# Mirrored matrix rows by way of DRAM, values by head in DRAM, and the order of the attention loads

## The chip, the cores and the metric

The kernel runs on one core of a Trainium2 chip. The metric is the device time of one execution in microseconds; the time before is the median of three runs. A profile of one further execution shows what each engine did: TensorE (PE, with its weight loads PEld), VectorE (DVE), ScalarE (ACT), GpSimd (POOL) and SyncE (SP), which here does nothing but issue DMAs. Line numbers (L941) are those of the kernel before.

## The reference

Two independent halves of 2048 tokens by 448 features each, whose results stand side by side in the output. Half A is a Fourier mixing layer, half B is attention with 16 heads of 28 features:

```python
# A: y = Re(DFT_seq(DFT_hidden(x))), with the four DFT matrices as inputs
a = einsum("bsd,ed->bse", x, dft_hid_re);  b = einsum("bsd,ed->bse", x, dft_hid_im)
y = einsum("ts,bse->bte", dft_seq_re, a) - einsum("ts,bse->bte", dft_seq_im, b)
# B: qkv = x @ wqkv, heads of 28
scores = einsum("bhqd,bhkd->bhqk", q, k) * 28 ** -0.5
o = einsum("bhqk,bhkd->bhqd", softmax(scores), v);  out = o (heads joined) @ wo
# result: concatenate([A, B], axis=-1), 2048 x 896, float32
```

The sequence matrices `dft_seq_re` and `dft_seq_im` (2048 x 2048 each, 16 MB) are inputs and not constants.

## The kernel before, in words

**The halves.** For B, queries, keys and values are computed first from `xb` and `wqkv`, each as a high and a low part, so that float32 precision is kept. Queries and keys go to a DRAM tensor `qk_d`, values to `v_d` (line 373), and each head reads back what it needs: keys in four pieces of 512 tokens (`head_loads`, L1183), queries in four pieces (`load_q`, L1197), values in one load. For every head the sixteen rows of score tiles (`kt` 0 to 15) are made 128 keys by 512 queries at a time (L1284), ACT exponentiates them (L1292), and PE multiplies them with the values (`quad`, L1261, matmuls at L1267). The row `kt` 0 of a head comes early (`first_tiles`, L1213): its maxima over the keys, made on DVE and POOL (L1230 to L1256), are subtracted inside all later rows of the head, so L1284 of a head cannot start before them. Buffers: five for key pieces, eight for query pieces (two heads), two for values.

**The sequence matrices.** A uses the symmetry of the DFT matrices to do a quarter of the work. Since the matrices are inputs, the kernel also checks on the chip that they do have that symmetry; if not, a slow general path runs at the end (it does not run with these inputs). The check reads both matrices whole, while attention runs, into six buffers `raw` of 128 x 1024: `rows_check` compares rows of one half with the other, `tokens_check` compares rows with the rows in descending order, `column_check` compares the first columns. The work is subtractions on DVE or POOL (`against`, L953) and a maximum on DVE (`largest`, L899).

**The descending rows.** `tokens_check` needs, for each of four blocks b and each matrix, rows in descending order. `Turned` (L935) reads them straight from the matrix with a negative row step, in four DMAs of 128 x 256 elements that POOL issues (L941). For block 0 the first row of each of the four groups is another one; it is read by two small DMAs over the same buffer, which wait for the four large ones (L946).

**The order of the work.** The whole program is written out by a planner (`Schedule`): each task has an engine, a key, a duration and what it depends on, and for each engine in turn the ready task with the lowest key is taken as soon as its buffers are free in the plan. Every engine then runs its list in that order on the chip. `soon` lowers the key by which a task is picked, but not the key by which buffers are handed out in turn. A task on SP is a DMA; the plan lets eight be in flight, and models their landing. `begun(key)` ties a load of the check to the head that the plan expects at that time: it may not be issued before that head reaches its fifth row of scores (`opened`, L1291).

**Values.** `values` (L775) makes them for eight heads at a time, 128 tokens after 128 tokens. Each result is copied with a one and three zeros behind each head's 28 columns (32 in all) into its own `kept` buffer, and stored by one DMA of 128 KB (L795). `head_loads` reads a head's 32 columns of all tokens (L1191).

Of the kernel before, what the change touches and what calls it, by code (L numbers as in the profile page):

```python
# [11 lines left out]
F32 = mybir.dt.float32  # L12
# [10 lines left out]
H = 16  # L23
# [12 lines left out]
SLACK_K, EARLY = 2.5, 8.0  # L36
# [3 lines left out]
T_FAR = 13.0  # L40
# [313 lines left out]
def tile_kernel(ctx, tc, xa, wre, wim, wd, xb, wqkv, wo, out):  # L354
# [18 lines left out]
    v_d = dram.tile([P, NT, H * VW], F32, name="vd")  # L373
# [401 lines left out]
    def values(ready, half):  # L775
        v_done[half] = []
        cols = slice(half * HV * DH, (half + 1) * HV * DH)
        for c in range(NC):
            for t in range(4):
                tok = slice(c * CH + t * P, c * CH + (t + 1) * P)  # L780
                o, pair = early_bank(), kept_s.slot()
                vs = lambda pair=pair: pair.t[:, 0, :HV * VW]
# [6 lines left out]
                def put(o=o, vs=vs):  # L789
                    v3 = vs().rearrange("p (h d) -> p h d", h=HV)  # L790
# [143 lines left out]

    class Turned(Stack):  # L935


        def __init__(self, part, b, key):
            self.raw = raw = raw_s.slot()
            src = (wre, wim)[part]  # L940
            at = lambda rows, cols, off, ap: far_dma(key, lambda: nc.gpsimd.dma_start(self.t[rows, cols], bass.AP(  # L941
                tensor=src.tensor, offset=src.offset + off, ap=[[tile_n, 4], *ap, [1, cols.stop - cols.start]])), T_FAR, d=0.7, deps=begun(key), use=[raw])
            q = H1 // 4
            self.ld = [at(slice(0, P), slice(i * q, (i + 1) * q), H1 + i * q + (P - 32 * b) * row_n, [[-row_n, 32]]) for i in range(4)]
            if not b:
                at = lambda cols, off: far_dma(key, lambda: nc.gpsimd.dma_start(self.t[0:P:32, cols], bass.AP(  # L946
                    tensor=src.tensor, offset=src.offset + off, ap=[[tile_n, 4], [1, cols.stop - cols.start]])), 3.0 + SLACK, d=0.6, deps=self.ld[:4], use=[raw])
                self.ld += [at(slice(0, H1 - P), H1 + P), at(slice(H1 - P, H1), 0)]
# [234 lines left out]
    def head_loads(h):  # L1183
        KT[h] = [kt_s.slot() for c in range(NC)]
        for c in range(NC):
            k = KT[h][c]
            got_k[h, c] = [dma(begins[h] - 34 - EARLY + (20 + c * P_H / NC if c else 0), lambda k=k, c=c: rows_of(
                k.t, 1, h * 2 * DH + DH, c * CH, (c + 1) * CH),
                size=84, extra=X_ROWS, n=2, slack=SLACK_K, deps=[*rows_ready(h, c, DH), *clears], use=[k])]
# [7 lines left out]
    def load_q(h, c, q):  # L1197
        return [dma(begins[h] - 33 - EARLY + c, lambda: rows_of(q.t, 0, h * 2 * DH, c * CH, (c + 1) * CH),
                    size=84, extra=X_ROWS, n=2, slack=SLACK_K, deps=[*rows_ready(h, c, 0), *clears], use=[q])]
# [290 lines left out]
def any_scores(tc, qk_d, v_d, on_d, wo, out, ks, qs, vs, kept, banks, new):  # L1490
# [20 lines left out]
    with tc.For_i(0, H, 1) as h:  # L1511
        with tc.For_i(0, S, CH) as c0:
# [16 lines left out]
            with tc.For_i(0, S, CH) as k0:  # L1529
                rows(k, h * 2 * DH + DH, (0, 0, 1), k0)  # L1530
                nc.gpsimd.dma_start(v, v_d[:, bass.ds(k0 // P, 4), bass.ds(h * VW, VW)])
# [85 lines left out]
```

## Time and profile before

| | |
|---|---|
| median of three runs | 743.26 us (742.86 to 743.95) |
| the profiled execution | 745.1 us, of which its span 743.5 us |
| granted TensorE clock over the span | 0.978 |
| busy | PE 710.5, ACT 610.9, DVE 507.3, POOL 375.8 us |
| DMA packets | 116160, of which 54470 under 512 bytes; 127.80 MB |
| DMA queue of SP | 109300 packets, 120.75 MB |
| DMA queue of POOL | 6784 packets, 6.14 MB |
| HBM | 96.64 MB read, 32.69 MB written |

The span is the time from the first to the last instruction in the trace. Busy time of PE is pipelined matmul time whose ends are modelled. A row of the stage tables names a stretch of the span and the busy time in it; a row of the chain of waits names when, for how long and on what the work that ended last was held up, followed back from the end.

### The profile page before, as it was taken

Reading aid. Unit: us, or ns where it says so; the run is one execution under the profiler, and the core shown is the slowest. Engines: PE = TensorE matmul, PEld = TensorE weight load, DVE = VectorE, ACT = ScalarE, POOL = GpSimd, SP = SyncE. Lnnn points to the kernel's source line nnn. Section 1 sums busy time; section 2 is a strip of 40 time slices with the busy share of each in tenths; the row PEclk is TensorE's granted clock in tenths of the full one; section 3 lists DMA queues with packets and bytes.
Section 4 is the critical chain, followed back from the end, with each engine's and each line's share of the span. In section 5 each row is a group of like instructions: output and inputs, shape, how many; then the busy total and the mean of one; then the engine's idle time right before and its main releaser. Section 6 shows DMA issues by size and latency. Waiting matters only on the chain.

```text
span 743.5 us, 12892 instructions
## 1 busy us (share of the span) xinstructions
PE 710.5 (96%) x4147; PEld 399.0 (54%) x4147; DVE 507.3 (68%) x864; ACT 610.9 (82%) x1232; POOL 375.8 (51%) x367
## 2 busy tenths in 40 slices
PE   9899999989999998899999999989989999999886
PEld 7697544444555544355545554535445554545765
DVE  6558637658868578687799776839888927423741
ACT  6315999968899989699999999979988999999141
POOL 7303314556464175553665356554898525547800
PEclk9999999998999999899999999989999999999989
DMA  8758539975779996888778599666352414232464
GB/s 289 251 196 221 147 80 224 193 162 151 169 200 242 257 192 177 200 216 217 203 195 228 151 243 220 161 194 200 103 141 78 101 50 124 62 107 51 109 190 181
DMA packets 116160, 127.80 MB, mean 172 GB/s; under 512 B 54470, under 2 KB 80728, under 8 KB 116084
## 3 DMA queue, kind: packets, MB, share of 16 engines
q1 hardware_dynamic: 109300, 120.75, 61.3%
q0 software_dynamic: 6784, 6.14, 3.7%
q8 instruction: 35, 0.57, 0.3%
q14 instruction: 41, 0.34, 0.2%
HBM read 96.64 MB, written 32.69 MB: 174 GB/s over the span
## 4 chain that ended last, share of the span: by engine, by line
PE 68%; ACT 9%; DMA 7%; POOL 6%; DVE 5%; issue 2%; SPq 1%; POOLq 0%; DVEq 0%; ACTq 0%
PE bank L1284 25%; PE bank L1267 25%; PE bank L687 10%; ACT kept L1292 7%; PE bank L867 3%; PE bank L1451 2%; PE bank L729 2%; DMA raw<-wre 2%; PE bank L1225 2%; DMA q<-qkd 1%; DMA kept<-kept 1%; POOL raw L953 1%; POOL kept L1256 1%; DMA kept<-ond 1%; DMA raw<-wim 1%
## 5 line engine op out<-in xcount | busy, mean ns | idle before, releaser
L1292 ACT ACTIVATE kept<-bank 128x512 f32<-128x512 f32 x960 | 499.7, 682 | 29.8 <-PE bank L1284 27.6
L1284 PE MATMUL bank<-q,k 98*128 98x512 f32 x960 | 304.5, 419 | 14.1 <-ACT kept L1292 8.0
L1284 PEld LDWEIGHTS bank<-q,k 98*128 98x128 f32 x960 | 174.1, 191 | 149.7 <-ACT kept L1292 106.3
L1267 PE MATMUL bank<-kept,v 128*32 128x512 f32 x2048 | 252.3, 611 | 0.0
L953 POOL TENSOR_TENSOR raw<-raw,raw 128x1024 f32<-128x1024 f32 (+3 forms) x54 | 112.1, 2081 | 53.8 <-DMA raw<-wre 29.6
L1267 PEld LDWEIGHTS bank<-kept,v 128*32 128x32 f32 x2048 | 54.4, 110 | 120.0 <-issue 114.3
L899 DVE TENSOR_REDUCE far<-raw 128x1 f32<-128x1024 f32 (+2 forms) x78 | 86.0, 1112 | 23.3 <-POOL raw L953 20.6
L1254 POOL CAST q<-mb 1x512 fp32r<-1x512 f32 x38 | 31.2, 830 | 109.4 <-DVE mb L1251 76.9
L1230 DVE STREAM_TRANSPOSE mb<-bank 128x512 f32<-128x512 f32 x64 | 43.9, 702 | 39.3 <-PE bank L1225 24.7
L1229 ACT ACTIVATE kept<-bank 128x512 f32<-128x512 f32 x64 | 39.5, 657 | 26.2 <-PE bank L1225 22.9
L1330 POOL TENSOR_TENSOR kept<-kept 128x512 f32<-128x512 f32 x16 | 20.8, 1301 | 77.6 <-DVE kept L1325 58.5
L1258 ACT ACTIVATE kept<-kept 128x512 f32<-128x512 f32 x64 | 46.0, 755 | 10.1 <-POOL kept L1256 5.0
L687 PE MATMUL bank<-big,whi 128*128 128x512 f32 x132 | 47.7, 402 | 1.7 <-DVE big L457 1.7
L1256 POOL TENSOR_TENSOR kept<-kept,mb 128x512 f32<-128x512 f32 x33 | 46.2, 1408 | 4.6 <-DVE mb L1251 1.6
L1251 DVE STREAM_TRANSPOSE mb<-am 128x512 f32<-128x512 f32 x64 | 42.9, 695 | 1.5 <-POOL q L1254 0.5
L1231 DVE TENSOR_REDUCE qm<-mb 128x16 f32<-128x512 f32 x64 | 41.7, 668 | 0.5
L687 PE MATMUL bank<-wd,big 128*128 128x224 f32 x288 | 41.8, 274 | 0.0
L687 PEld LDWEIGHTS bank<-wd,big 128*128 128x128 f32 x288 | 39.2, 191 | 3.4 <-issue 0.8
L953 DVE TENSOR_TENSOR raw<-raw,raw 128x1024 f32<-128x1024 f32 (+2 forms) x30 | 35.2, 1178 | 0.7 <-DMA raw<-wim 0.6
L1256 DVE TENSOR_TENSOR kept<-kept,mb 128x512 f32<-128x512 f32 x31 | 34.8, 1131 | 0.2
L687 PEld LDWEIGHTS bank<-big,whi 128*128 128x128 f32 x132 | 24.6, 189 | 12.5 <-issue 4.2
L1225 PE MATMUL bank<-q,k 84*128 84x512 f32 x64 | 27.6, 433 | 3.2 <-ACT kept L1292 2.3
(173 smaller groups left out, 788.3 us busy)
## 6 DMA issues: line engine op xcount, KB each, us to landing
raw<-wre SPq DMA_DIRECT2D x64, 256.0 KB
raw<-wim SPq DMA_DIRECT2D x64, 256.0 KB
qkd<-kept SPq DMA_DIRECT2D x40, 256.0 KB
k<-qkd SPq DMA_DIRECT2D x64, 112.0 KB
q<-qkd SPq DMA_DIRECT2D x64, 112.0 KB
kept<-xb SPq DMA_DIRECT2D x16, 256.0 KB
vd<-kept SPq DMA_DIRECT2D x32, 128.0 KB
v<-vd SPq DMA_DIRECT2D x16, 256.0 KB
```

The costliest lines, as they stand in the source:

```text
L687: nc.tensor.matmul(o.t[:, :cols], w(), x(), start=(i == 0), stop=(i == n - 1))
L899: far_done.append(dve(key, lambda: nc.vector.tensor_reduce(far[rows, part, n:n + 1], t(), axis=AX.X if len(t().shape) == 2 else AX.XY, op= ...
L953: return sch.add(d, at, lambda g: eng[g].tensor_tensor(xv(), xv(), yv(), op=op), deps=[*x.ld, *y.ld, *deps], use=[x.raw, y.raw])
L1225: m = pe(key, lambda e, o=o, q=q: nc.tensor.matmul(o.t, KT[h][0].t[:KR, :P], q.t[:KR, :], start=True, stop=True), deps=[*lq, *got_k[h, 0], ...
L1230: t = dve(key, lambda o=o, tm=tm: nc.vector.transpose(tm.t, o.t), 0.73, deps=[m], acq=[tm], use=[o], lock=[o], own=RAW_S)
L1231: rs.append(dve(key, lambda tm=tm, c=c: nc.vector.tensor_reduce(qm.t[:, 0, c * NT:(c + 1) * NT], tm.t.rearrange("p (j r) -> p j r", r=32), ...
L1251: t = dve(key, lambda mb=mb, c=c: nc.vector.transpose(mb.t, f32(am.t)[:, c * NT:(c + 1) * NT].unsqueeze(2).to_broadcast([P, NT, 32])), 0.7 ...
L1256: sh = sch.add({"DVE": 1.15, "POOL": 1.4}, key, lambda e, s=s, mb=mb: eng[e].tensor_tensor(s.t, s.t, mb.t, op=ALU.add), deps=[t, made[c]], ...
L1258: shown.append(act(key, lambda s=s: nc.scalar.activation(s.t, s.t, AF.Exp, scale=SCALE), ACT_S, deps=[sh], use=[s.pair]))
L1267: nc.tensor.matmul(o.t[c * VW:(c + 1) * VW, :], VT[h].t[:, kt // 4, kt % 4, :], tiles[c].t, start=(kt == 0), stop=(kt == NT - 1))
L1284: m = pe(key, lambda e, o=o, q=q, kt=kt: nc.tensor.matmul(o.t, KT[h][kt // 4].t[:KM, kt % 4 * P:(kt % 4 + 1) * P], q.t[:KM, :], start=True ...
L1292: es[h, kt].append(act(key - 20, lambda o=o, p=p: nc.scalar.activation(p.t, o.t, AF.Exp, scale=SCALE), deps=[m], use=[o, p.pair]))
```

## The change

**Mirrors.** A new function `mirror` makes, for each of the two sequence matrices, a copy of 4 x 128 rows of 1024 elements in DRAM (`t_d`), in descending order. Four DMAs that SP issues do it, each with 16 x 127 runs of 64 elements (256 bytes), so that the runs of a row lie on different DMA engines; two small ones fill the first row of each group. Their keys are 60 and 110 us. `Turned` then reads its block as four plain loads of 32 rows each, issued by SP after the mirror has landed. POOL issues none of these loads any more.

**Values by head.** `v_d` is ordered by partition, head, tile and column. Four results share one `kept` buffer and are stored by one DMA of 512 KB in runs of 512 bytes; a head's load is 128 runs of 2 KB.

**Loads of attention.** Key, query and value loads get `soon=PRIOR` (40 us); `EARLY`, which took 8 us off the keys of the key and query loads, becomes 0. The lines left out adapt the slow path.

```diff
-SLACK_K, EARLY = 2.5, 8.0
+SLACK_K, EARLY, PRIOR = 2.5, 0.0, 40.0
-T_FAR = 13.0
+MIRROR_AT = 60.0, 110.0
-    v_d = dram.tile([P, NT, H * VW], F32, name="vd")
+    v_d = dram.tile([P, H, NT, VW], F32, name="vd")
...
+            pair, put_all = kept_s.slot(), []
+            v4 = lambda pair=pair: pair.t.rearrange("p a b -> p (a b)").rearrange("p (h t d) -> p h t d", h=HV, t=4)
             for t in range(4):
...
-                b = dve(key - 45, put, 0.55, deps=[end], use=[o, pair])
-                v_done[half].append(dma(key - 20, lambda vs=vs, c=c, t=t: nc.sync.dma_start(
-                    v_d[:, 4 * c + t, half * HV * VW:(half + 1) * HV * VW], vs()), 128, deps=[b], use=[pair]))
+                put_all.append(dve(key - 45, put, 0.55, deps=[end], use=[o, pair]))
+            v_done[half].append(dma(key - 20, lambda v4=v4, c=c: nc.sync.dma_start(
+                v_d[:, half * HV:(half + 1) * HV, 4 * c:4 * c + 4, :].rearrange("p h t d -> p h (t d)"),
+                v4().rearrange("p h t d -> p h (t d)")), 512, deps=put_all, use=[pair]))
...
+    t_d = [dram.tile([4, P, H1], F32, name=f"mirror{i}") for i in range(2)]
+    mirrored = [[], []]
+    def mirror(part, key):
+        src, dst, n = (wre, wim)[part], t_d[part], H1 // 16
+        for a in range(4):
+            mirrored[part].append(dma(key + 6 * a, lambda a=a: nc.sync.dma_start(
+                bass.AP(tensor=dst.tensor, offset=dst.offset + (a * P + 1) * H1, ap=[[n, 16], [H1, P - 1], [1, n]]),
+                bass.AP(tensor=src.tensor, offset=src.offset + a * tile_n + H1 + (P - 1) * row_n, ap=[[n, 16], [-row_n, P - 1], [1, n]])),
+                900, 1.0, deps=begun(key)))
+        for c0, c1, off in ((0, H1 - P, H1 + P), (H1 - P, H1, 0)):
+            mirrored[part].append(dma(key, lambda c0=c0, c1=c1, off=off: nc.sync.dma_start(
+                bass.AP(tensor=dst.tensor, offset=dst.offset + c0, ap=[[P * H1, 4], [1, c1 - c0]]),
+                bass.AP(tensor=src.tensor, offset=src.offset + off, ap=[[tile_n, 4], [1, c1 - c0]])), 16, 1.0, deps=begun(key)))
...
-            at = lambda rows, cols, off, ap: far_dma(key, lambda: nc.gpsimd.dma_start(self.t[rows, cols], bass.AP(
-                tensor=src.tensor, offset=src.offset + off, ap=[[tile_n, 4], *ap, [1, cols.stop - cols.start]])), T_FAR, d=0.7, deps=begun(key), use=[raw])
...
+            self.ld = [dma(key, lambda a=a: nc.sync.dma_start(self.t[32 * a:32 * a + 32], t_d[part][a, 32 * b:32 * b + 32]),
+                           128, slack=SLACK, deps=[*begun(key), *mirrored[part]], use=[raw]) for a in range(4)]
...
-            got_k[h, c] = [dma(begins[h] - 34 - EARLY + ..., size=84, extra=X_ROWS, n=2, slack=SLACK_K, deps=..., use=[k])]
+            got_k[h, c] = [dma(begins[h] - 34 - EARLY + ..., size=84, extra=X_ROWS, n=2, slack=SLACK_K, soon=PRIOR, deps=..., use=[k])]
...
-            v.t.rearrange("p c t d -> p (c t) d"), v_d[:, :, h * VW:(h + 1) * VW]), extra=1.0, deps=v_done[h // HV], use=[v])]
+            v.t.rearrange("p c t d -> p (c t) d"), v_d[:, h]), soon=PRIOR, deps=v_done[h // HV], use=[v])]
...
+        mirror(part, MIRROR_AT[part])
```

The query loads (`load_q`) change as the key loads do, and `mirror` is called in the loop over the two matrices, between `rows_check` and `tokens_check`.

More of the change, by code (lines that the diff above doesn't have):

```diff
@@ L778, in values @@
         for c in range(NC):
+            pair, put_all = kept_s.slot(), []
+            v4 = lambda pair=pair: pair.t.rearrange("p a b -> p (a b)").rearrange("p (h t d) -> p h t d", h=HV, t=4)
             for t in range(4):
                 tok = slice(c * CH + t * P, c * CH + (t + 1) * P)
-                o, pair = early_bank(), kept_s.slot()
-                vs = lambda pair=pair: pair.t[:, 0, :HV * VW]
+                o = early_bank()
                 seq = products(lambda k: lz(x_h, k, tok), lambda k: lz(x_l, k, tok), lambda: lz(x_3, tok),
@@ L787, in values, with put @@
                             {3 * k: [xb_ready[c, k], ready[k], *ready[4:][:k // 3]] for k in range(4)}, v_last)
-                def put(o=o, vs=vs):
-                    v3 = vs().rearrange("p (h d) -> p h d", h=HV)
+                def put(o=o, t=t, v4=v4):
+                    v3 = v4()[:, :, t]
                     nc.vector.tensor_copy(v3[:, :, :DH], o.t[:, :HV * DH].rearrange("p (h d) -> p h d", h=HV))
@@ L939, in __init__ @@
             self.raw = raw = raw_s.slot()
-            src = (wre, wim)[part]
-            at = lambda rows, cols, off, ap: far_dma(key, lambda: nc.gpsimd.dma_start(self.t[rows, cols], bass.AP(
-                tensor=src.tensor, offset=src.offset + off, ap=[[tile_n, 4], *ap, [1, cols.stop - cols.start]])), T_FAR, d=0.7, deps=begun(key), use=[raw])
[L943 to L948, printed above, removed]
+            self.ld = [dma(key, lambda a=a: nc.sync.dma_start(self.t[32 * a:32 * a + 32], t_d[part][a, 32 * b:32 * b + 32]),
+                           128, slack=SLACK, deps=[*begun(key), *mirrored[part]], use=[raw]) for a in range(4)]
     sub_if = lambda yes: ALU.subtract if yes else ALU.add
@@ L1188, in head_loads @@
                 k.t, 1, h * 2 * DH + DH, c * CH, (c + 1) * CH),
-                size=84, extra=X_ROWS, n=2, slack=SLACK_K, deps=[*rows_ready(h, c, DH), *clears], use=[k])]
+                size=84, extra=X_ROWS, n=2, slack=SLACK_K, soon=PRIOR, deps=[*rows_ready(h, c, DH), *clears], use=[k])]
         v = VT[h] = v_s.slot()
         got_v[h] = [dma(begins[h] - 4, lambda: nc.sync.dma_start(
-            v.t.rearrange("p c t d -> p (c t) d"), v_d[:, :, h * VW:(h + 1) * VW]), extra=1.0, deps=v_done[h // HV], use=[v])]
+            v.t.rearrange("p c t d -> p (c t) d"), v_d[:, h]), soon=PRIOR, deps=v_done[h // HV], use=[v])]
         flat = lambda: v.t.rearrange("p c t d -> p (c t d)")
@@ L1198, in load_q @@
         return [dma(begins[h] - 33 - EARLY + c, lambda: rows_of(q.t, 0, h * 2 * DH, c * CH, (c + 1) * CH),
-                    size=84, extra=X_ROWS, n=2, slack=SLACK_K, deps=[*rows_ready(h, c, 0), *clears], use=[q])]
+                    size=84, extra=X_ROWS, n=2, slack=SLACK_K, soon=PRIOR, deps=[*rows_ready(h, c, 0), *clears], use=[q])]
     before = {}
@@ L1530, in any_scores @@
                 rows(k, h * 2 * DH + DH, (0, 0, 1), k0)
-                nc.gpsimd.dma_start(v, v_d[:, bass.ds(k0 // P, 4), bass.ds(h * VW, VW)])
+                nc.gpsimd.dma_start(v, v_d[:, bass.ds(h, 1), bass.ds(k0 // P, 4), :].rearrange("p o t d -> p (o t) d"))
                 for kt in range(4):
```

## The prediction

> **What bounds the kernel now.** I read the page first, then the busy time of every engine head by head (a head runs from its first exponential of line 1292 to the next head's), then the chain of waits in the heads that stand out.
>
> ```profile
> span 743.5 us, 12892 instructions
> PE 710.5 (96%) x4147; PEld 399.0 (54%) x4147; DVE 507.3 (68%) x864; ACT 610.9 (82%) x1232; POOL 375.8 (51%) x367
> ```
>
> The share of PE says little, since its ends are modelled. The heads say more. Columns: stretch, its length, then busy time of PE, PEld, DVE, ACT and POOL, the granted clock, the DMA share and GB/s.
>
> ```profile
> 102.60:136.50 33.90, 33.87 (x194) 14.73 (x193) 24.21 (x35) 33.73 (x70) 13.10 (x11) 1.00 0.77 184
> 136.50:180.50 44.00, 40.07 (x224) 19.32 (x224) 30.49 (x48) 35.56 (x71) 27.88 (x23) 0.92 0.72 163
> 180.50:218.70 38.20, 38.17 (x241) 20.21 (x241) 29.47 (x52) 34.46 (x70) 18.20 (x10) 1.00 0.75 187
> 294.60:340.50 45.90, 40.89 (x216) 19.68 (x217) 35.50 (x51) 37.02 (x75) 24.70 (x18) 0.93 0.81 201
> 340.50:378.10 37.60, 36.69 (x215) 18.59 (x213) 28.32 (x41) 35.13 (x72) 20.89 (x21) 1.00 0.84 206
> 378.10:415.80 37.70, 37.70 (x216) 19.03 (x216) 34.87 (x44) 36.07 (x75) 20.31 (x14) 1.00 0.75 203
> 452.50:496.00 43.50, 40.68 (x213) 19.47 (x212) 31.57 (x48) 36.65 (x74) 28.55 (x28) 0.92 0.70 181
> 533.70:576.20 42.50, 39.91 (x243) 20.85 (x241) 34.89 (x59) 37.14 (x77) 39.05 (x39) 0.96 0.43 119
> sum 623.00, PE 605.72 PEld 309.49 DVE 442.60 ACT 573.35 POOL 334.41; mean PE 37.86 PEld 19.34 DVE 27.66 ACT 35.83 POOL 20.90
> ```
>
> The sixteen heads fill 623.0 of the 743.5 us. A quiet head takes 37.7 us with ACT busy for 36.1 of it, so there ACT sets the pace and nothing that this change touches can shorten it. Four heads are longer: head 2 (from 136.5) by 6.3 us, head 6 (294.6) by 8.2, head 10 (452.5) by 5.8, head 12 (533.7) by 4.8. In all four ACT was busy no longer than about 37 us and the granted clock is 0.92 to 0.96: PE and ACT both stood still. These 25.1 us are the room for any change outside ACT.
>
> Head 2, by the chain of waits (start, length, what):
>
> ```profile
> 151.69 8.23 DMA raw<-wre
> ...
> 161.64 2.40 POOL raw L953
> ...
> 165.28 2.05 DVE kept L1256
> ...
> 167.36 0.63 ACT kept L1258
> ...
> 168.53 1.77 PE bank L1284 x3
> ```
>
> ```profile
> POOL raw L941 <- DVE far L899: 10.0, 4, 3.9
> ...
> POOL raw L946 <- DMA raw<-wre: 8.2, 1, 8.2
> ...
> POOL raw L946 <- DMA raw<-wim: 6.8, 1, 6.8
> ```
>
> POOL issues the mirrored loads of the check (line 941), and for the first block of each matrix it must then wait for them before it issues the two small ones on top (line 946). While it stands, the check's subtraction (L953), and the maxima behind it (L1254, L1256) that let the next head's scores start, stand too. The same wait for the second matrix, 6.8 us, lies in the head from 340.5, which shows no excess: it costs nothing.
>
> Head 6 has another chain:
>
> ```profile
> 262.90 9.22 DMA q<-qkd
> ...
> 286.34 2.17 DMA raw<-col
> ...
> 293.31 1.89 DVE raw L1015
> ...
> 297.99 1.50 POOL q L1254
> ...
> 299.53 1.65 PE bank L1284 x3
> ```
>
> ```profile
> 258.63 3.56 SPq L918 DMA_DIRECT2D raw<-wre  x6
> ```
>
> The last query piece lands 9.2 us after its issue, and it is issued behind six matrix loads. From its landing at 272.1 to the last maxima row (L1254 ends at 299.5) it takes 27 us, in which the column check sits in DVE's queue.
>
> In head 10 a matrix load stands ahead of the maxima on DVE:
>
> ```profile
> 461.35 5.70 DMA raw<-wim
> ```
>
> **The change part by part.** All sums are against the profiled execution, 743.5 us of span and 745.1 us in all; the median of the runs shown, 743.26, is 1.8 lower, and that is taken off at the end.
>
> *Mirrored loads leave POOL.* Thirty-two loads and four small ones go:
>
> ```profile
> L941 POOL DMA_DIRECT2D raw<-wre x16 | 11.0, 694 | 4.2 <-DVE far L899 4.1
> L941 POOL DMA_DIRECT2D raw<-wim x16 | 10.9, 685 | 6.1 <-DVE far L899 5.9 <-issue 0.3
> ```
>
> That is 21.9 us of POOL's time plus its waits. POOL is busy for 51%, so the issue time alone is worth 0; its cover is POOL's idle time, and without it it would be at most those 21.9 us. What counts is the 8.2 us wait at line 946. Without it, head 2 can fall to the quiet 37.7 us. Bounds: 0 (L953 waits for the same data, by another load) and −6.3 us. I take −6.0, because the chain runs through this wait alone, and the mirrored copy is begun a head before block 0 is loaded. Next to be late is then ACT itself.
>
> *The loads come back on SP.* Thirty-two plain loads of 128 KB (four for each of eight blocks) and twelve DMAs that write the mirrors. SP issues in order, and the wait for a free `raw` buffer now stands ahead of key and query loads:
>
> ```profile
> SPq L1163 <- PE bank L1284: 92.9, 52, 8.2
> SPq L918 <- DVE far L899: 23.2, 13, 4.6
> ```
>
> SP already waits 23.2 us for these buffers in 13 waits, 1.8 us each; POOL's four waits of 10.0 us move here. What queues behind them are query and key loads, and PE's first score tiles wait for those. Bounds: 0 and +10.0; I take +1: SP is a queue with idle time of its own, and a wait of 1.8 us hurts only where the next load is already late.
>
> *The mirrors.* For each matrix, four DMAs of 520 KB from DRAM to DRAM, each 16 x 127 = 2032 runs of 256 bytes, and two tiny ones. The nearest rows are the kernel's own reversed copies (line 574): three DMAs of about 1027 runs of 512 bytes, and three of about 1024 runs of 224 bytes, issued back to back.
>
> ```profile
> 222.28 2.63 SPq L574 DMA_DIRECT2D wt<-wd  x3
> ...
> 227.59 5.34 SPq L574 DMA_DIRECT2D xt<-xa  x3
> ```
>
> The second stretch is paced by the queue: 1.78 us for each DMA. By bytes a mirror DMA is the same 520 KB, 1.8 us; by runs it is twice that, 3.5 us. I take 2.6, nearer neither end: 10.5 us of all 16 engines for a matrix, 21 us together. Where it falls:
>
> ```profile
> 75.00:100.00 25.00, 25.00 (x152) 12.55 (x152) 14.97 (x22) 24.24 (x50) 9.36 (x7) 1.00 0.49 125
> 100.00:125.00 25.00, 24.97 (x148) 11.04 (x144) 16.26 (x28) 24.83 (x52) 4.83 (x5) 1.00 0.67 166
> 125.00:150.00 25.00, 24.77 (x138) 10.37 (x130) 16.91 (x24) 24.58 (x51) 16.00 (x10) 1.00 0.94 201
> ```
>
> The first mirror may start when head 0 reaches its fifth row of scores, near 75 us; 51% of the next 25 us is free, 12.7 us, and hides it. The second waits for head 1, near 112 us, where 33% and then 6% are free: some 6 us push into the loads behind. Bounds: 0 (there is slack of a head) and +8.2 (a stall like that of head 6); I take +2. The Trainium skill ("DMA: Bandwidth & Descriptors", Specifications) says that transfers under 512 bytes lose the line rate to a read-modify-write, which speaks against 256-byte runs; by its 27 GiB/s for an engine, 520 KB would take an estimated 1.1 us at line rate and 2.3 us at half of it. The rows here, 1.8 to 3.5 us, agree that these runs are slow.
>
> *Values by head.* Sixteen loads with 2048 runs of 128 bytes become loads with 128 runs of 2 KB, and 32 stores of 128 KB become 8 of 512 KB. DVE waits little for values, PE not at all:
>
> ```profile
> DVE ok L1194 <- DMA v<-vd: 3.8, 3, 1.9
> ```
>
> Bounds −3.8, and +1.8, because the first head's values now wait for a whole store of 512 KB, which by the row of the reversed copies takes 1.78 us. I take 0: the 3.8 us are DVE's, which idles for a third of the span, and only the first head's load follows straight on its stores.
>
> *Key, query and value loads first.* Their places in the planner's order move up by 32 us (40 of PRIOR less the 8 of EARLY; the values by 40), so they pass the matrix loads that are ready at the same time. They cannot pass a full buffer. In head 6 the six loads that were issued ahead are 3.6 us of issue and more of landing. Bounds 0 and −8.2; the column check still sits in DVE's queue, so I take −3. In head 10 the chain's 5.7 us is a matrix load, whose queue gets lighter by POOL's share and worse by its lower rank: bounds 0 and −5.8, I take −2. Head 12 has no such load in its DMA share of 0.43: 0.
>
> Sum: −6.0 + 1 + 2 + 0 − 3 − 2 = −8.0. 745.1 − 8.0 = 737.1 in the profile, less 1.8: 735 us.
>
> **The rivals.**
>
> *The wait only moves.* POOL stands at L953 in place of L946, because the planner's order puts the subtraction just behind the expected landing and the real one is later. For it:
>
> ```profile
> POOL raw L953 <- DMA raw<-wre: 29.6, 6, 13.0
> ```
>
> Against it: in head 2 there is a single such wait on the chain. The planner may also find nothing to reorder, since keys and queries wait for buffers and not for their rank (92.9 us above); then the priority does not do what it says. Then −6.0 and −5 become about −1, and the costs +3 shrink to +0.5: 742.5 us.
>
> *Queries late behind the mirrors.* This one ends slower. Head 2's queries are issued at 98.8 to 102.8 us, and its last first tile starts at 113.6:
>
> ```profile
> 102.76 0.38 SPq L1164 DMA_DIRECT2D q<-qkd  x1
> ...
> L1225 PE MATMUL bank<-q,k x8: 391/398/502, 63.5 to 113.6; 84*128 84x512 f32 x8
> ```
>
> From there to the maxima head 6 took 27 us, 17 without the 10 or so that its column check holds (286.3 to 297); so the slack before head 2 starts at 136.5 is at most 6 us. Head 3's queries come in the busiest stretch (0.94), behind the second mirror. If the mirrors take 3.5 us each (14 us a matrix) and the displaced matrix loads delay queries by over 6 us, heads 2 and 3 stall as head 6 did, 8.2 us each. Minus 6 for the removed wait and with nothing won in heads 6 and 10, that is 743.3 + 16.4 − 6 − 1 = 752.7, or 748.6 if one stall is half as long: about 750 us. Against it: the first mirror meets a half-empty queue.
>
> *All three DMA stalls go.* Queries land early enough for heads 6 and 10 to be quiet: −6.3 − 8.2 − 5.8 + 2 = −18.3, so 725 us. For it: each of these chains holds a DMA; against it: the column check and the maxima share DVE.
>
> **How the numbers follow.** Main case 45%, own range 729 to 742; wait only moves 17%; queries late 20%; all stalls gone 18%. Changes of 0.2%, 1.5 us, are about what a measurement here tells from none: faster is below 741.8, slower above 744.8. Main gives 40/4/1 in hundredths to faster/same/slower, the first rival 6/8/3, the second 0/1/19, the third 18/0/0: 0.64, 0.13, 0.23. The range runs from 722, a little under the third case, to 751, a little over the second.
>
> **What would show it.** Right: no POOL wait at the mirrored loads, head 2 near 38 us at a clock of 1.00, the `raw` waits of SP longer than 23.2 us, query landings under 9 us in head 6. The mirror DMAs should keep SP for 7 to 14 us a matrix. Wrong: a POOL wait at L953 in head 2 as long as the one removed; first tiles (L1225) of head 2 well after 114 us, with a clock below 1.00 in heads 2 and 3; or new excess in heads that are quiet now, because the planner's whole order shifts with its keys.

## The result, and the profile after

The changed kernel takes 722.25 us, the median of four runs (720.57 to 725.41), beside 743.44 us for the kernel before on the same chip (742.86 to 743.95): a ratio of 0.972, 95% interval 0.968 to 0.976. That is 21.2 us faster where 8 were forecast. The profiled execution took 720.6 us. The top of its page, and the line on the chain that ended last:

```profile
span 719.0 us, 12825 instructions
PE 700.0 (97%) x4147; PEld 394.4 (55%) x4147; DVE 498.3 (69%) x861; ACT 609.5 (85%) x1232; POOL 348.6 (48%) x334
...
PE 86%; ACT 6%; DMA 2%; DVE 2%; SPq 1%; POOL 1%; issue 1%; ACTq 0%; POOLq 0%
```

ACT is busy as long as before (609.5 against 610.9 us) while the span fell by 24.5, so ACT lost idle time. PE lost 14.0 us of idle time, and 10.5 us of busy time for the same 4147 matmuls, beside a granted clock of 0.997 where it was 0.978. The same shows head by head (stretch, length, then PE, PEld, DVE, ACT, POOL, granted clock, DMA share, GB/s). These are heads 2, 3, 6, 7, 10 and 12 of the kernel after; the stretches run from a head's first exponential to the next head's. Rows of a changed kernel carry its own line numbers: L964, L920, L1174, L1295 and L1303 of the kernel after are L953, L918, L1163, L1284 and L1292 of the kernel before.

```profile
137.00:174.60 37.60, 37.59 (x243) 20.32 (x243) 24.14 (x47) 34.85 (x71) 17.97 (x14) 1.00 0.74 204
174.60:212.60 38.00, 37.82 (x241) 20.17 (x240) 31.22 (x57) 34.62 (x70) 18.10 (x12) 1.00 0.84 212
...
288.30:327.10 38.80, 38.77 (x215) 18.94 (x215) 31.88 (x49) 36.51 (x73) 21.69 (x16) 1.00 0.94 223
327.10:363.80 36.70, 36.70 (x216) 18.92 (x214) 28.35 (x42) 35.62 (x73) 20.25 (x13) 1.00 0.81 222
...
439.30:478.30 39.00, 38.64 (x216) 18.85 (x215) 32.65 (x46) 36.51 (x75) 23.62 (x21) 1.00 0.64 184
...
515.70:555.90 40.20, 38.77 (x243) 20.29 (x241) 35.99 (x60) 36.85 (x77) 34.17 (x36) 1.00 0.40 121
...
sum 603.00, PE 598.04 PEld 307.93 DVE 433.90 ACT 570.54 POOL 306.72; mean PE 37.38 PEld 19.25 DVE 27.12 ACT 35.66 POOL 19.17
```

Head 2 went from 44.0 to 37.6 us, head 6 from 45.9 to 38.8, head 10 from 43.5 to 39.0, head 12 from 42.5 to 40.2, and the granted clock is 1.00 in each of them, where it was 0.92 to 0.96. In a quiet head such as head 7 PE's busy time fills the whole stretch (36.70 us) and ACT's does not (35.62), and on the chain PE holds 86% and ACT 6%; that ACT sets the pace of a quiet head, as the prediction had it, is not shown. The sixteen heads lost 20.0 us (623.0 to 603.0). What comes behind the last head's last exponential, the tail, lost 4.3 more, from 743.5 − 686.7 = 56.8 to 719.0 − 666.5 = 52.5.

The waits of POOL and of SP in the kernel after (who waited for what: us, times, longest):

```profile
POOL raw L964 <- DMA raw<-wre: 14.2, 6, 3.4
...
POOL raw L964 <- DMA raw<-mirror: 1.1, 1, 1.1
```

```profile
SPq L1174 <- PE bank L1295: 103.2, 59, 8.2
...
SPq L920 <- DVE far L901: 12.3, 11, 4.2
```

The 8.2 and 6.8 us that POOL waited at L946 are gone, and POOL waits for mirrored rows once, 1.1 us. SP's wait for a free `raw` buffer (L920 on L901, which is L899 of the kernel before) did not grow, it fell from 23.2 to 12.3 us. The mirror DMAs and the plain loads on SP's queue (ns minimum/median/maximum of the issue, first and last start):

```profile
L944 SPq DMA_DIRECT2D mirror<-wre x4: 600/641/2146, 74.6 to 87.2; - x4
L944 SPq DMA_DIRECT2D mirror<-wim x4: 599/612/620, 116.9 to 156.7; - x4
...
L958 SPq DMA_DIRECT2D raw<-mirror x32: 308/419/1487, 161.9 to 455.3; - x32
```

And the stretches in which the mirrors are made:

```profile
75.00:100.00 25.00, 25.00 (x154) 10.12 (x152) 9.30 (x16) 23.78 (x50) 5.77 (x5) 1.00 0.80 196
100.00:125.00 25.00, 24.25 (x140) 10.83 (x140) 16.93 (x27) 23.59 (x48) 6.42 (x5) 1.00 0.66 173
125.00:150.00 25.00, 25.00 (x166) 13.33 (x159) 16.64 (x29) 23.38 (x48) 13.77 (x10) 1.00 0.74 201
```

The DMA engines, busy for 0.49 of the first 25 us before, are now busy for 0.80: the first mirror fits into what was free. From 125 to 150 the share fell from 0.94 to 0.74, and the four DMAs of the second mirror are spread over 40 us.

### The profile page after: what moved, and what is told of

Read it like the earlier page. It is cut to its first block, busy times and chain, and to the rows that moved or that the text cites. A ratio compares the mean times of both kernels' runs of the same rounds, so it can differ in the third digit from the quotient of the medians.

```text
span 719.0 us, 12825 instructions
## 1 busy us (share of the span) xinstructions
PE 700.0 (97%) x4147; PEld 394.4 (55%) x4147; DVE 498.3 (69%) x861; ACT 609.5 (85%) x1232; POOL 348.6 (48%) x334
## 3 DMA queue, kind: packets, MB, share of 16 engines
q0 software_dynamic: 2048, 1.86, 1.1%
## 4 chain that ended last, share of the span: by engine, by line
PE 86%; ACT 6%; DMA 2%; DVE 2%; SPq 1%; POOL 1%; issue 1%; ACTq 0%; POOLq 0%
PE bank L1295 33%; PE bank L1278 31%; PE bank L687 13%; ACT kept L1303 4%; PE bank L869 2%; PE bank L729 2%; PE bank L1463 2%; PE bank L1236 2%; DMA kept<-ond 1%; SPq L1145 1%; ACT kept L1240 1%; DMA kept<-kept 0%; DMA kept<-xb 0%; POOL kept L1133 0%; DVE big L457 0%
## 5 line engine op out<-in xcount | busy, mean ns | idle before, releaser
L1303 ACT ACTIVATE kept<-bank 128x512 f32<-128x512 f32 x960 | 499.0, 680 | 20.3 <-PE bank L1295 18.6
L1295 PE MATMUL bank<-q,k 98*128 98x512 f32 x960 | 299.6, 414 | 4.5 <-ACT kept L1303 4.3
L1295 PEld LDWEIGHTS bank<-q,k 98*128 98x128 f32 x960 | 171.5, 188 | 136.5 <-ACT kept L1303 105.8
L1278 PE MATMUL bank<-kept,v 128*32 128x512 f32 x2048 | 246.2, 598 | 0.0
L964 POOL TENSOR_TENSOR raw<-raw,raw 128x1024 f32<-128x1024 f32 (+3 forms) x52 | 101.2, 1953 | 54.3 <-DVE raw L964 21.2
L901 DVE TENSOR_REDUCE far<-raw 128x1 f32<-128x1024 f32 (+2 forms) x78 | 86.0, 1111 | 6.3 <-POOL raw L964 3.5
L1265 POOL CAST q<-mb 1x512 fp32r<-1x512 f32 x40 | 33.2, 838 | 96.9 <-DVE mb L1262 67.2
L1240 ACT ACTIVATE kept<-bank 128x512 f32<-128x512 f32 x64 | 39.5, 664 | 26.7 <-PE bank L1236 23.2
L1267 POOL TENSOR_TENSOR kept<-kept,mb 128x512 f32<-128x512 f32 x39 | 54.4, 1405 | 4.1 <-ACT kept L1303 1.2
L1269 ACT ACTIVATE kept<-kept 128x512 f32<-128x512 f32 x64 | 45.9, 757 | 2.5 <-POOL kept L1267 2.2
L964 DVE TENSOR_TENSOR raw<-raw,raw 128x1024 f32<-128x1024 f32 (+3 forms) x32 | 38.0, 1188 | 9.0 <-DMA raw<-wre 8.9
L1332 DVE STREAM_TRANSPOSE kept<-kept 128x512 f32<-128x512 f32 x16 | 11.3, 709 | 42.9 <-ACT kept L1330 42.9
L1267 DVE TENSOR_TENSOR kept<-kept,mb 128x512 f32<-128x512 f32 x25 | 29.2, 1175 | 0.2
```

The source lines that it names most:

```text
L901: far_done.append(dve(key, lambda: nc.vector.tensor_reduce(far[rows, part, n:n + 1], t(), axis=AX.X if len(t().shape) == 2 else AX.XY, op= ...
L964: return sch.add(d, at, lambda g: eng[g].tensor_tensor(xv(), xv(), yv(), op=op), deps=[*x.ld, *y.ld, *deps], use=[x.raw, y.raw])
L1240: made.append(act(key, lambda o=o, s=s: nc.scalar.activation(s.t, o.t, AF.Copy), deps=[m], use=[o, s.pair], lock=[o]))
L1267: sh = sch.add({"DVE": 1.15, "POOL": 1.4}, key, lambda e, s=s, mb=mb: eng[e].tensor_tensor(s.t, s.t, mb.t, op=ALU.add), deps=[t, made[c]], ...
L1269: shown.append(act(key, lambda s=s: nc.scalar.activation(s.t, s.t, AF.Exp, scale=SCALE), ACT_S, deps=[sh], use=[s.pair]))
L1278: nc.tensor.matmul(o.t[c * VW:(c + 1) * VW, :], VT[h].t[:, kt // 4, kt % 4, :], tiles[c].t, start=(kt == 0), stop=(kt == NT - 1))
```

## The experiments

The change has three parts that can be made one at a time: the mirrors, the values by head, and the loads of attention first. Seventeen kernels were run beside the kernel before, whose median in these comparisons lay between 743.8 and 745.3 us. The lengths of heads come from one profiled execution of each kernel, up to 8 us off its median, so what several kernels agree in says more than one length. Four theories stood against each other. **A**: POOL's wait at L946 is the loss, and a kernel without it has both head 2 and head 7 short. **B**: the rank of the attention loads is what matters. **C**: each edit only makes the planner write another order, and the time is the luck of that order. **D**: a wait costs only where the written order puts the check's work ahead of the next head's maxima on DVE.

### One part alone, and the wait alone

`e_mirror` has the hunks of `mirror` and `Turned` of the diff and nothing else; `e_values` has the hunks of `values`, `v_d` and the load of values; `e_first` has these:

```diff
-SLACK_K, EARLY = 2.5, 8.0
+SLACK_K, EARLY, PRIOR = 2.5, 0.0, 40.0
@@ key and query loads @@
-size=84, extra=X_ROWS, n=2, slack=SLACK_K, deps=...
+size=84, extra=X_ROWS, n=2, slack=SLACK_K, soon=PRIOR, deps=...
@@ load of values @@
-extra=1.0, deps=...
+extra=1.0, soon=PRIOR, deps=...
```

`e_wait_on_sp` is the kernel before with the two small loads of block 0 issued by SP, so that POOL doesn't wait for the large ones:

```diff
-at = lambda cols, off: far_dma(key, lambda: nc.gpsimd.dma_start(...), 3.0 + SLACK, d=0.6, deps=self.ld[:4], use=[raw])
+at = lambda cols, off: dma(key, lambda: nc.sync.dma_start(...), 16, slack=SLACK, deps=self.ld[:4], use=[raw])
```

> The mirrors alone; values and the rank of the attention loads as before. Theory A (POOL's wait for the descending rows was the main cost): head 2 falls from 44.0 to about 38 us, heads 6 and 10 stay long, 737 us or a little less. Theory B (the rank of the attention loads did most of it): 740 us or more. Theory C (each edit makes the planner write another order, and the long heads come and go with it): any of the heads 2, 6, 10, 12 may change, also those in which no descending row is loaded.

> Key, query and value loads first, alone. Theory A: heads 6 and 10 shrink by 3 and 2 us, head 2 keeps its POOL wait of about 8 us: 738 us. Theory B: 728 us or less, with heads 6 and 10 near 38 us. Theory C: long heads in other places than before.

> Values by head alone. Theories A and B: 743 us, within 2 us, all four long heads as before. Theory C: a long head appears or goes though neither POOL's loads nor the ranks change.

> The kernel before, but the two small loads of block 0 (line 946) are issued by SP, so that the wait for the four large ones stands on SP and no longer on POOL; no mirrors. Theory A: head 2 falls to about 38 us, 737 us, unless SP's queue holds queries back by the same 8 us (then 743 or more). Theory B: 743 us. Theory C: heads other than 2 change as well.

Measured: the mirrors alone 732.45 us, ratio 0.983 (0.978 to 0.988); the loads first alone 740.04, 0.994 (0.991 to 0.998); the values by head alone 734.63, 0.988 (0.983 to 0.993); the wait alone 737.20, 0.991 (0.988 to 0.994). Each part helps by itself, the values too, for which theories A and B had 743 us; and the mirrors alone give more than A had for them. Where the wait alone goes, in heads 2, 6 and 7 of `e_wait_on_sp`:

```profile
137.00:174.00 37.00, 36.76 (x225) 18.31 (x225) 26.18 (x45) 35.02 (x72) 27.55 (x23) 1.00 0.87 191
...
290.20:336.70 46.50, 41.22 (x216) 19.96 (x217) 35.81 (x51) 37.03 (x75) 24.94 (x18) 0.93 0.80 198
336.70:373.70 37.00, 36.90 (x216) 18.88 (x214) 30.08 (x42) 34.93 (x72) 21.37 (x21) 1.00 0.91 221
```

Head 2 is quiet at 37.0 us and head 6, which the wait did not concern, is as long as before. In `e_first` the wait is still there, head 2 takes 36.6 us all the same, and head 7 pays. Its row, and its chain of waits:

```profile
332.40:375.70 43.30, 39.30 (x215) 19.36 (x214) 30.17 (x39) 36.10 (x73) 23.45 (x24) 0.92 0.76 188
```

```profile
346.67 1.14 DVE far L899
...
348.09 2.03 POOL raw L941 x3
350.12 9.73 DMA raw<-wim
359.88 0.04 POOLq L946
```

So the wait for the second matrix, which cost nothing in the order before, costs 6 us in another order. Which of the two heads pays is a matter of the order (so far D), that one of them pays is not (A). In the profiles of the eleven kernels in which POOL has this wait, heads 2 and 7 together take 79.7 to 89.9 us; in the eight without it, 71.7 to 74.4.

### Another order of the same work

`e_told` is the kernel before with `T_FAR` 21 in place of 13, so that the planner expects POOL's loads later. `e_shift` and `e_shift_73` change the key of the check's work alone, which is 75 us in both kernels; `e_after_shift` and `e_after_shift_73` do the same to the kernel after:

```diff
-CHECK_AT, CHECK_STEP = 75.0, 90.0
+CHECK_AT, CHECK_STEP = 77.0, 90.0
```

> The kernel before with T_FAR 21 in place of 13: the same loads by POOL and the same wait at line 946; only the planner is told that these loads land 8 us later, so it writes another order. Theory A (POOL's wait costs by itself): about 743 us, head 2 at 44 us. Theory D (the wait costs only where the written order has the check's maximum, which depends on POOL, ahead of the next head's maxima on DVE): head 2 near 38 us with a POOL wait of 5 us or more still there, 734 to 739 us.

> A control: the kernel before with CHECK_AT 77 in place of 75, so that all work of the check has keys 2 us later; nothing else. Theories A and B: 743 us within 2 us, the same four long heads. Theories C and D: long heads move, 730 to 750 us, in either direction.

> The kernel before with the planner's key of the checks at 73 us in place of 75, as a second control beside the one at 77 (753.7 us): the same instructions in another order. Theory C, that the kernel before is one draw among written orders of one work: anywhere from 733 to 754 us. If the order before is a good one for its work and a shift only harms: 744 or more. Heads 2 and 7 together 79 to 90 us (A: POOL's wait is still there), whichever of the two pays.

> The kernel after with the planner's key of the checks at 77 us in place of 75, the pair of the control that gave 753.7 us. If the change takes stalls away whatever the order: 722 to 733, that is 20 us or more under its pair, with heads 2 and 7 together 73 to 76 us. If the kernel after only met a lucky order (C): 735 or more, with long heads (43 us or more) as before. Of the 9.5 us that the same shift cost before, a kernel without stalls on a DMA should lose less than half: 722 to 727.

> The kernel after with the planner's key of the checks at 73 us, the pair of 743.5 us for the kernel before. The pairs so far are 21 us (75) and 25.6 us (77) apart. If the change is worth that whatever the order: 718 to 726. If a third of it is luck of the order: 727 or more. Heads 2 and 7 together 73 to 76 us.

| key of the check | before | after | difference |
|---|---|---|---|
| 73 us | 743.53 (741.21 to 747.87) | 722.72 (721.25 to 726.86) | −20.8 |
| 75 us | 743.44 (742.86 to 743.95) | 722.25 (720.57 to 725.41) | −21.2 |
| 77 us | 753.73 (751.74 to 757.47) | 728.16 (725.55 to 729.75) | −25.6 |

The medians of a row come from different chips. By the ratios against the kernel before on the same chip, times 743.8 us, the differences are 21.3, 20.8 and 21.7 us.

`e_told` took 740.26 us, 0.992 (0.989 to 0.996); in its profile head 2 is still 43.4 us long, so telling the planner of the later landing didn't clear that head, which D had asked for. Yet heads 6 and 10 are shorter in it than before, 41.3 and 37.7 us, with every load ranked as before: an order alone can do that. Theory C is right in one thing: 2 us in the key of work that is done anyway cost 9.5 us beside the kernel before on the same chip (744.22), ratio 1.011 (1.004 to 1.017). As the cause of this result it falls: in three orders of either kernel the change is worth 20.8 us or more. No kernel beat the one after; its order at 73 us is as fast. The shift to 77 cost the kernel after 5.9 us by the medians and 7.0 by the ratios, more than half of what it cost before, where under half was expected.

### Two parts together

`e_no_mirror`, `e_no_first` and `e_no_values` each leave one part of the change out.

> The changed kernel without the mirrors: values by head and attention loads first, descending rows by POOL as before. If the parts add up, 743.8 - 9.2 - 3.8 = 731 us. Theory A: 735 us or more, since POOL's wait is back. Theory D: anywhere from 725 to 738 us, and the POOL waits at the small loads are back whether or not head 2 is long.

> The mirrors and the values by head, with the loads ranked as before. If the parts add (before 743.8, mirrors alone -11.4, values alone -9.2): 723.2 us, so the rank is worth 1 us of the whole. My recorded sum, which gave the rank of the loads 5 of its 8 us: at least 727. If the gain of every edit is mainly the luck of another written order (theory C), the time need not follow the sum: anywhere from 722 to 735, with one or two heads of 41 us or more. In all theories in which POOL's wait for the descending rows costs what it did in the earlier runs (A), heads 2 and 7 together take 73 to 75 us, as in the four runs that have no such wait.

> The mirrors and the loads first, with the values by block of rows as before (128-byte pieces, two stores a block). If the parts add: 743.8 - 11.4 - 3.8 = 728.6 us. My recorded sum, which gave the values nothing: as the whole change, 722. Theory C: 722 to 735. Heads 2 and 7 together 73 to 75 us (A).

Measured: without the mirrors 733.48 us, 0.984 (0.978 to 0.990); without the loads first 730.22, 0.985 (0.980 to 0.989); without the values by head 728.05, 0.980 (0.976 to 0.984). With the single parts, that gives every combination. What a part adds, in us, is the difference of two ratios times 743.8:

| added | to the kernel before | to one other part | to both others | mean |
|---|---|---|---|---|
| mirrors | −12.6 | −11.1 on loads first, −2.5 on values | −8.7 | −8.7 |
| values by head | −8.9 | +1.3 on mirrors, −8.0 on loads first | −5.6 | −5.3 |
| loads first | −4.2 | −2.6 on mirrors, −3.3 on values | −9.5 | −4.9 |

The intervals of the ratios are some ±0.5%, 3.7 us; that makes an estimated ±5 us for a cell and ±2.6 for a mean of four, so a single cell says little. The expectation for `e_no_first`, 723.2 by adding the parts, was missed by 7 us: the loads first seem worth more when the other two are in. Theory A's 735 us or more for `e_no_mirror` was missed by 1.5. Now where: lengths from the profiled executions, in us.

| kernel | start of head 0 | heads 2 + 7 | head 6 | head 10 | head 12 | tail |
|---|---|---|---|---|---|---|
| before | 63.7 | 81.6 | 45.8 | 43.5 | 42.5 | 56.8 |
| mirrors | 65.2 | 72.8 | 42.7 | 41.3 | 43.2 | 54.2 |
| loads first | 66.7 | 79.9 | 41.9 | 39.0 | 43.6 | 54.3 |
| values | 62.7 | 83.3 | 39.4 | 40.5 | 42.6 | 53.3 |
| mirrors, loads first | 67.9 | 71.7 | 42.7 | 38.9 | 40.9 | 54.9 |
| mirrors, values | 63.5 | 73.9 | 45.9 | 43.2 | 38.9 | 53.0 |
| loads first, values | 62.3 | 84.2 | 41.4 | 38.5 | 44.0 | 52.0 |
| all three | 63.5 | 74.3 | 38.8 | 38.9 | 40.2 | 52.5 |

Heads 2 and 7 together take 71.7 to 74.3 us in all kernels with the mirrors, 79.9 to 84.2 without. With `e_wait_on_sp` (74.0) on the short side, and the two shifted kernels before on the long side, this is theory A, and its size is 9.1 us. Head 10 is 38.5 to 39.0 us long wherever the loads go first, 40.5 to 43.5 elsewhere: theory B for that head, 3.3 us on the mean, though `e_told` reached 37.7 us there by its order. Head 6 is 2.2 us shorter on the mean where the loads go first, but from 2.0 longer to 7.1 shorter in single pairs. In `e_no_first` heads 6 and 10 are as long as before:

```profile
287.40:333.30 45.90, 40.47 (x215) 19.57 (x216) 36.93 (x49) 37.27 (x75) 25.94 (x20) 0.93 0.82 207
...
443.30:486.50 43.20, 40.64 (x215) 18.98 (x214) 36.49 (x51) 36.58 (x74) 22.20 (x21) 0.96 0.62 175
```

### The price of the mirrors

`e_mirror_twice` is the kernel after in which each large mirror DMA is followed by the same copy into a DRAM tensor that nobody reads. The loads of the mirrored rows wait for the spare copies too.

```diff
+spare = [dram.tile([4, P, H1], F32, name=f"spare{i}") for i in range(2)]
-for a in range(4):
+for a, dst in [(a, d) for a in range(4) for d in (t_d[part], spare[part])]:
```

> The changed kernel with each of the eight large mirror DMAs done twice, the second time into a DRAM tensor that nobody reads: the price of the mirrors by itself. By the prediction's step (10.5 us of the DMA queue for a matrix, +2 us on the path): +2 us, 724 us. By the rival (queries late behind the mirrors): +8 us or more, heads 2 and 3 long, 730 us. If the first half-empty queue hides them all: 722 us, within 1.5.

Measured: 743.61 us, 21.4 above the kernel after, which no case had foreseen. The profile is that of its slowest execution (748.9 us). Heads 0 to 4 together take 185.1 us against 188.3 in the kernel after, and head 5 starts earlier, at 247.3 us against 251.8. What the second copy does to SP's queue, and when the reversed copies of L574 come (their first and last start in the kernel after are 216.5 and 220.1 us for `wt<-wd`):

```profile
L945 SPq DMA_DIRECT2D spare<-wre x4: 1832/1942/2891, 74.1 to 109.3; - x4
L945 SPq DMA_DIRECT2D spare<-wim x4: 1727/3704/4649, 130.8 to 183.0; - x4
```

```profile
L574 SPq DMA_DIRECT2D wt<-wd x4: 595/612/1842, 254.3 to 269.1; - x4
L574 SPq DMA_DIRECT2D xt<-xa x4: 562/640/3911, 271.0 to 309.3; - x4
```

A copy right behind another holds SP for 1.9 and 3.7 us (medians). The reversed copies come 38 us later, but not because SP was held up until then. The queries of head 5 are issued from 209.7 us here and from 209.1 in the kernel after; there the reversed copies follow them, here they stand behind the queries of head 6:

```profile
209.67 0.32 SPq L1176 DMA_DIRECT2D q<-qkd  x1
...
254.33 0.63 SPq L574 DMA_DIRECT2D wt<-wd  x1
```

```profile
209.13 0.32 SPq L1174 DMA_DIRECT2D q<-qkd  x1
...
216.50 4.68 SPq L574 DMA_DIRECT2D wt<-wd  x4
```

So the planner, which knows of the second copies, wrote another order. Where the reversed copies are now (stretches of 25 us, then what POOL and PE waited for):

```profile
250.00:275.00 25.00, 24.50 (x134) 14.00 (x133) 13.49 (x17) 20.82 (x43) 11.61 (x8) 1.00 1.00 240
275.00:300.00 25.00, 16.17 (x87) 8.16 (x85) 14.50 (x25) 14.21 (x28) 7.72 (x6) 0.82 0.93 252
```

```profile
POOL raw L966 <- DMA raw<-wre: 18.2, 2, 13.0
```

```profile
PE bank L1238 <- DMA q<-qkd: 5.0, 2, 3.2
```

The DMA engines are full, POOL waits 13.0 us for matrix rows and PE waits for queries: heads 5 and 6 take 53.3 and 46.7 us. It is a stall of the kind that the second rival told of, but over 60 us after the last mirror is issued (183.0), in the stretch of the reversed copies. One set of mirrors costs nothing that shows. The 21 us of the second set are its price together with that of another order; this run doesn't part the two.

### The values taken apart

Each of these is the kernel before with one thing changed. `e_values_load` orders `v_d` by head and loads 2 KB runs, but keeps the 32 stores (now of 128-byte runs); TensorE, VectorE, ScalarE and GpSimd get the same instructions in the same order. `e_values_store` keeps the layout and the load, and stores four tiles with one DMA. `e_values_four` has the order of `e_values_store` on these four engines, but issues each store as four DMAs. `e_values_told` changes the planner's figure alone.

```diff
@@ e_values_load @@
-v_d[:, 4 * c + t, half * HV * VW:(half + 1) * HV * VW], vs())
+v_d[:, half * HV:(half + 1) * HV, 4 * c + t, :], vs().rearrange("p (h d) -> p h d", h=HV))
-v_d[:, :, h * VW:(h + 1) * VW]), extra=1.0,
+v_d[:, h]), extra=1.0,
@@ e_values_store @@
+v_d[:, 4 * c:4 * c + 4, half * HV * VW:(half + 1) * HV * VW], v4()..., 512, deps=put_all
@@ e_values_four, against e_values_store @@
+[nc.sync.dma_start(v_d[:, 4 * c + t, ...], v4()[:, t]...) for t in range(4)], 512, deps=put_all
@@ e_values_told @@
-v_d[:, :, h * VW:(h + 1) * VW]), extra=1.0, deps=...
+v_d[:, :, h * VW:(h + 1) * VW]), deps=...
```

> The kernel before with the values laid out by head in DRAM, but stored as before by 32 stores (now of 128-byte pieces) and with the planner told the same: TensorE, VectorE, ScalarE and GpSimd get the same instructions in the same order. If the time of the loads' small pieces was what the values by head took away: 734 to 738 us (-6 to -9). If it was the stores or the order: 742 to 746, as before; if the small pieces only move from the load to the store and cost there as much, the same. Head 2 stays near 44 us in both, since POOL's wait for the descending rows is in place.

> The kernel before with one store of values to a block of tokens (8 in all, 512 KB each) in place of four, the layout in DRAM and the load as before. If the 24 stores less on SP's queue were it: 734 to 738 us, with the start of head 0 at 62.7 us or less (before 63.7). If it was the load: 742 to 746. If it is the order (theory C), anything from 733 to 752, since the planner writes another one here too.

> The kernel before with nothing changed but the planner's figure for the load of values (no extra microsecond): the same instructions and the same pieces in another order. Theory C (the gain of the values by head was an order): 733 to 740. If it was work: 742 to 746, or up to 753, as the control at 77 us gave.

> The kernel with one store of values to a block of tokens (734.2 us), in which each of these stores is issued as four DMAs of 128 KB, one behind the other: the same order on all engines, and as many stores on SP's queue as in the kernel before. If the 24 stores were the cost: 741 us or more, by 24 issues of 0.6 us on SP, as the mirrors' own issues took. If the order was the gain: 732 to 737.

Measured: the load 740.84 us, ratio 0.991 (0.987 to 0.996); the stores 734.22, 0.987 (0.984 to 0.990); the same with four DMAs each 738.18, 0.993 (0.991 to 0.996); the figure alone 744.73, 1.003 (1.000 to 1.005). The load's seven times lie apart (732.3 to 744.5), and their median lies between the two ranges expected, so its share is the least sure; by the ratio it is 6.5 us, by the medians 3.1, with no other order to explain it. Of the stores' 9.9 us, 4.8 come back when 32 stores are issued in the same order, so they are the price of 24 DMAs, give or take 3 us by the intervals; the other 5.1 come with the order, or with the 8 buffers in place of 32 that bring it. The queue rows of `e_values_store` and `e_values_four`:

```profile
L796 SPq DMA_DIRECT2D vd<-kept x8: 391/422/596, 41.3 to 216.4; - x8
```

```profile
L796 SPq DMA_DIRECT2D vd<-kept x32: 332/401/1479, 37.4 to 218.9; - x32
```

At 0.4 us each, 24 issues are 9.6 us of SP. My expectation took 0.6 us for an issue, and set all or nothing where it was half. The early start of head 0 that I had tied to fewer stores (62.7 us or less) did not come: 63.5. And the two halves don't add: 6.5 us for the load and 9.9 for the stores, but 8.9 for both (`e_values`).

## Why the prediction was wrong

The forecast was −8.0 us; −21.2 came, near the third rival, "all three DMA stalls go", forecast at 725 us with 18%. That heads 2, 6 and 10 all go quiet came as it said (−18.0 us, forecast −20.3); that the time is so near is in part luck, since head 12 and the tail, which it didn't have, gave 6.6 us more. By places, in the profiled executions, whose difference is 24.5 us:

| term | forecast | came |
|---|---|---|
| head 2, POOL's wait | −6.0 | −6.4 |
| head 6, queries | −3.0 | −7.1 |
| head 10, matrix load | −2.0 | −4.5 |
| head 12 | 0 | −2.3 |
| SP's queue and the mirrors | +3.0 | nothing to be seen |
| tail | not in the sum | −4.3 |

The start and the other heads add up to +0.1.

**POOL's wait: right, by its mechanism and its size.** Head 2 fell as forecast, and the wait alone is worth 6.9 us (ratio 0.991). "The same wait for the second matrix costs nothing" was true only of the order before: in `e_first`, `e_values`, `e_no_mirror`, `e_values_store` and `e_values_four` head 7 took 43 to 46 us in place of head 2. The first rival, that the wait only moves to the subtraction, did not come: its waits for `wre` fell from 29.6 to 14.2 us, the longest from 13.0 to 3.4.

**SP's queue, +1, and the mirrors, +2: the steps that failed in the sum.** The mirrors as a part are worth −8.7 us on the mean, not −3, though the wait alone is 6.9: no cost of theirs shows. SP's buffer waits fell, where I had forecast longer ones. A mirror DMA of 2032 runs kept SP for 0.6 us, or 2.1 where one was issued right behind another: about 4 us for the first matrix and 2.5 for the second, not 7 to 14. I had taken the pace of the reversed copies, which are issued back to back; the mirrors' keys lie 6 us apart. I had also read one of the two rows only: the copies with runs of 224 bytes took 0.88 us for some 1020 runs (2.63 us for three), so by runs too a mirror DMA came to 1.8 us and not to 3.5. The doubled copies brought the pace back: 0.65 + 1.94 us for two of `wre`, 0.61 + 3.70 for two of `wim`, an estimated 1.3 to 2.2 us each. The price on the DMA engines was no more than I took: their share from 75 to 100 us rose by 0.31, that is 7.8 us with all else that moved there, where I had 10.5 for a matrix. By the Trainium skill ("DMA: Bandwidth & Descriptors", Specifications) four mirror DMAs are an estimated 4.5 us at line rate and 9.0 at half of it. The 7.8 us lie between, and as the stretch holds other transfers too, no run here decides. The rival "queries late behind the mirrors" did not come: the last first tile of head 2 starts at 113.4 us, before at 113.6. The doubled copies met a stall of its kind, in other heads and in another order.

**Values by head, 0: the other step that failed.** I costed the wait that the trace named (3.8 us of DVE for values) and took the rest as hidden. The runs give −5.3 us on the mean of the combinations (an estimated ±2.6), and −8.9 alone, where my bound was −3.8: 24 issues on SP and 2048 small runs a load are time of the queue that feeds the queries and the checks, and no row of waits for values shows that. How this time reaches the path is not shown.

**Loads first, −5: right in sum, and for a half-right reason.** The part is worth −4.9 on the mean. For head 6 I held the landing of the last query piece to be late, and the column check to stay in DVE's queue. The issue of the four query pieces of head 6, before and after:

```profile
L1163 SPq DMA_DIRECT2D q<-qkd x1: 320/320/320, 262.5 to 262.5; - x1
```

```profile
L1174 SPq DMA_DIRECT2D q<-qkd x4: 314/327/334, 248.3 to 251.7; - x4
```

Before, the last piece is issued 32.1 us ahead of the head's start (294.6), behind six matrix loads; after, 36.6 us ahead (288.3), with the other three. That is 4.5 us won. From its issue to its score tile it takes 9.7 us before and 11.3 after, so landing did not get faster, and "under 9 us" was wrong. From that tile to the last of the maxima it takes 27.2 us before and 19.8 after: 7.4 us won, since the last maxima (done at 282.8 us) no longer stand behind the column check. Its subtractions begin at 285.4 us now, and one of the two that ran on DVE (L1004, which is L1015 of the kernel after) has gone to POOL:

```profile
L1015 POOL TENSOR_TENSOR raw<-raw 1x512 f32<-1x512 f32 x1 | 2.2, 2234 | 0.1
```

Together 4.5 − 1.6 + 7.4 = 10.3 us: the last maxima were 4.8 us behind the head's start and are now 5.5 ahead of it. I had held an order that the planner writes anew for a fact of the kernel. Nor is this the work of the rank alone: with the values by head alone head 6 takes 39.4 us.

**What I did not cost: the clock, head 12 and the tail.** The four long heads stand at a granted clock of 0.92 to 0.96. Here is head 2 of the kernel before, cut where PE stops and where the clock changes (columns as in the stage tables):

```profile
164.80:168.30 3.50, 0.02 (x1) 0.00 (x0) 3.47 (x3) 0.94 (x2) 3.50 (x2) 1.00 0.45 133
168.30:175.10 6.80, 6.58 (x22) 2.57 (x23) 6.59 (x10) 5.20 (x11) 6.16 (x6) 0.50 0.35 113
175.10:180.50 5.40, 5.40 (x37) 3.37 (x37) 4.72 (x6) 5.14 (x11) 4.01 (x5) 1.00 0.62 160
```

PE stands for 3.5 us, and in the 6.8 us behind that the granted clock is 0.50: 22 matmuls in 6.8 us, where 37 follow in 5.4. By an estimate, half of 6.8 us is lost, 3.4, so of this head's excess of 6.3 us about half is the stall and half the slow clock behind it. Heads 6 and 10 have the same 6.8 us at 0.50 (from 298.0 and 489.2 us), head 12 has 3.4 us (from 543.8); the heads of the kernel after have none. A stall does not always bring it: in the tail of the kernel after PE stands for 2.4 us (from 696.1) at a clock of 1.00. No run changes the clock alone.

The tail, before and after, and its last matmuls on the chain:

```profile
686.70:743.50 56.80, 45.39 (x220) 37.58 (x218) 26.03 (x60) 14.68 (x37) 18.59 (x22) 0.92 0.54 160
```

```profile
666.50:719.00 52.50, 42.70 (x220) 34.98 (x218) 27.37 (x60) 14.41 (x36) 18.68 (x22) 0.99 0.59 174
```

```profile
720.89 16.13 PE bank L1451 x70
```

```profile
698.46 14.59 PE bank L1463 x70
```

The same 70 matmuls take 1.5 us less of the 4.3, at a higher clock. On the same chain the waits for DMAs add up to 15.8 us before and 12.4 after; why they are shorter stays open. The tail is 52.0 to 53.3 us in the four kernels of the table with the values by head, 54.2 to 56.8 in the four without, but the clock parts them as well: 0.97 to 0.99 in the first four, 0.92 to 0.94 in the others. `e_values_told`, whose work is that of before, has 53.7 us at 0.97, and `e_values_load`, with the values by head, 57.1 at 0.91. So the values are not shown to shorten the tail. Open are also what shortens head 12, how the other 5.1 us of the merged stores split between the order and the fewer buffers, and whether the mirrors truly add only 2.5 us to the values alone.

## What to carry to other kernels

Where a planner writes the order of in-order queues, shift one of its keys by a little in both kernels before a gain of under 10 us is believed: here that alone moved the time by 9.5 us, and only pairs of runs told the change from the order. A cost that lies in idle time of an in-order queue (issues on SP, small runs) need not be zero because nobody is seen to wait for it. Count a stall of PE together with the slow clock behind it, where the profile shows one. And doubling a piece of work to price it prices the planner's new order too, unless the lists of the engines stay the same.

## What the runs showed of the hardware

A DRAM-to-DRAM copy in 2032 runs of 256 bytes held SP for 0.6 us where it was issued alone, and 1.9 to 3.7 us (medians) right behind another: the same work, so the length of an issue is no measure of the transfer. Eight of these copies, 4.2 MB, passed beside attention without a cost that shows in the heads. And where POOL waits for DMAs that it has just issued, it stands until they have landed, 6 to 11 us in the profiles here. After stalls of 2.3 to 5.0 us of PE the granted clock was 0.50 for 3.4 or 6.8 us in the four long heads of the kernel before.
